# Block attention and a mixture of experts on one core: the first steps reordered, constants on GpSimd, two weight loads on its queue

## The chip, the cores and the metric

The kernel runs on one core of one Trainium2 chip. The metric is the device time of a run in microseconds; the time given is the median of several runs.

## The reference

Attention over q, k, v of shape (4, 8, 768, 64): each query sees the keys within 16 positions and, for each of 24 blocks of 32, one summary (the maximum of the block's keys, with the mean of its values). The result, 3072 tokens of 512, goes through a mixture of 16 experts in 4 groups, one expert for each token.

```python
k_sum = k.reshape(B, H, nb, block, D).max(axis=3)
v_sum = v.reshape(B, H, nb, block, D).mean(axis=3)
scores_l = where(abs(i - j) < 16, scale * q @ k.T, -1e9)
scores_s = scale * q @ k_sum.T + log(32)
a = softmax(concat([scores_l, scores_s]))
x = a @ concat([v, v_sum])           # then (B*S, H*D)
g = argmax(x @ w_group); e = argmax(x @ w_expert[g])
out = p_g * p_e * (relu(x @ w1[g, e]) @ w2[g, e])
```

## The kernel before

**Attention.** The 32 heads are worked on in 16 pairs, `idx`; a pair takes three steps `n`, with four tiles of 64 queries from each head. `PLAN` (line 49) lists, for each of the three steps, the pieces of work in their order: `s` the scores (eight products on TensorE, then a mask pass `ss` on VectorE, L794), `e` the exponentials on ScalarE (L803), `t` the transposes of the probabilities of two steps before, `v` the products with the values of three steps before, `p0` to `p4` the preparation of k and q of the next pair (`prep`, L740: `p0`, `p1` transpose k, with copies into `kw` on ScalarE and VectorE, L763; `p2`, `p3` transpose q into `qt` on ScalarE, L757; `p4` copies the borders and reduces the block maxima on VectorE, L771 to L777), `m0` and `m1` the means of the values (`means`, L720) and `l0` to `l3` the routing logits of pairs further back. Each engine works through its own instructions in the order in which they were written, and the scores of the first step of a pair need all of its `p` pieces.

`means` in its first part multiplies the 12 value tiles with the matrix `stair`; 24 rows of block means result in `vp`. Its second part multiplies `vp` with `same`, which copies the means to the partitions from 96 on, and six GpSimd copies (L737) put them into the value tile `va`. Row 120 of `va` holds zeros, set once for each of the four buffers by `init_last` on GpSimd (L676).

**Loads.** `load_qk` (L629) loads k and q of a pair in one DMA each of 384 KB, `load_vw` the values in six DMAs (two of 192 KB, four of 44 KB) in pieces of 256 bytes. SyncE issues all of these. At the start it issues k and q of the pairs 0 and 1, the values of 0 and 1, and k and q of 2. `keep_warm` (L655) puts products with zeros on TensorE. For the steps 0 to 2 the means of pair 0 are written behind the step: after `n` = 1 its first part, after `n` = 2 its second. After `n` = 0 come the value memsets of the other three buffers and `router.consts` (L163), which makes the constants of the routing, `lower`, `ones` and `seen` by VectorE among them.

**Experts.** Tokens are gathered by indirect DMAs that GpSimd issues (L1041), and written by scatters (L1081). Weights come by `load_w` (L1012) in two halves of 1 MB: w1 (`w1r`) and w2 (`w2r`), both issued by SyncE. They are split into a high and a low part: a cast on ScalarE (`w1h`, `w2h`, L1034) and a subtraction on VectorE. `hook` in `block_attention_then_moe` (L1357) starts the first region while attention still runs: the first gathers at step last - 4, w2 at last - 2. The unit region follows: `weights` loads w1 and w2 of unit 0 once its number is known, `tokens` then issues the gathers of `xd` (`gather2(0)`) and, later, those of `ohr` (`gather2(1)`). `logits` copies the transposed tokens into `xT` (L847): part 0 on ScalarE, part 1 on VectorE.

Of the kernel before, what the change touches and what calls it, by code (L numbers as in the profile page):

```python
# [8 lines left out]
F32 = mybir.dt.float32  # L9
# [5 lines left out]
ALU = mybir.AluOpType  # L15
# [35 lines left out]
        ["s", "p3", "l3", "t", "v", "l0", "m0", "e"]]  # L51
LAG = {"l0": 1, "l1": 2, "l2": 2, "l3": 2}
# [10 lines left out]
GATHER_AT, W2_AT, X_AT = 4, 2, 1  # L63
# [6 lines left out]
AHEAD, LATE_AHEAD, SLOT_AHEAD, VECTOR_NS = 300, 1500, 800, 85  # L70
# [64 lines left out]
class Router:  # L135
# [27 lines left out]
    def consts(self):  # L163
# [12 lines left out]
        V.tensor_single_scalar(self.lower, self.lower, 0.0, op=ALU.is_gt)  # L176
        self.ones = pool.tile([P, P], BF16, name="ones")
        V.memset(self.ones, 1.0)
# [3 lines left out]
        self.ioe = iota([P, E], [[1, E]], -E, 0, "ioe")  # L182
        self.io32 = iota([32, E], [[1, E]], 0, 0, "io32")
# [8 lines left out]
        V.memset(self.seen, 0.0)  # L192
# [181 lines left out]
    def slots(self, name, col, nt, step, c0):  # L374
# [7 lines left out]
        def columns(values):  # L382
# [3 lines left out]
            for j0, eq in zip(groups, eqs):  # L386
# [8 lines left out]
                yield from self.pause(SLOT_AHEAD)  # L395
# [190 lines left out]
def attention(tc, q, k, v, w_group, w_expert, ident, x_dram, ps, router, hook):  # L586
# [24 lines left out]
    with ExitStack() as st, ExitStack() as nat_st:  # L611
# [62 lines left out]
        def init_last(i):  # L674

            nc.gpsimd.memset(va_ring[i][96:NR, :, :, 0:D], 0.0)  # L676

        for i in range(NVA):
            init_va(i)
        qk[1] = load_qk(1)  # L680
        load_vw(0)
        init_last(0)
# [4 lines left out]
        for cs, key in ((slice(0, QT), 0), (before, -PAD), (behind, QT)):  # L687
            nc.gpsimd.iota(mask[:, 0, cs], pattern=[[1, cs.stop - cs.start]], base=key, channel_multiplier=0,
                           allow_small_or_imprecise_dtypes=True)
        pi = cst.tile([P, 3], I32, name="place_i")  # L690
# [27 lines left out]
        same = cst.tile([P, NBLK], F32, name="same")  # L718

        def means(idx, part):  # L720
# [10 lines left out]
            else:  # L731
                T.matmul(out=t[KW:NC, 0:P], lhsT=same, rhs=vps.pop(idx), start=True, stop=True)
                vr = wk.tile([NC, 1, 2, D], F32, name="vr")
                V.tensor_copy(out=vr[KW:NC].rearrange("p a h d -> p (a h d)"), in_=t[KW:NC, 0:P])  # L734
                n = 2
                for i in range(0, NQT, n):
                    nc.gpsimd.tensor_copy(out=va[KW:NC, i:i + n, :, 0:D], in_=vr[KW:NC].broadcast_to([NBLK, n, 2, D]))  # L737
# [99 lines left out]
        def logits(idx, part):  # L837
            b, a = order[idx]
            x = xs[b]
            if part < 2:  # L840
# [6 lines left out]
                (V.tensor_copy if part else nc.scalar.copy)(  # L847
# [27 lines left out]
        keep_warm(5)  # L875
# [5 lines left out]
        for i in range(4):  # L881
            V.tensor_copy(out=same[32 * i:32 * i + 32], in_=ident[32 * i:32 * i + 32, 32 * i:32 * i + NBLK])
# [5 lines left out]
        for n in range(NG + 3):  # L888
# [4 lines left out]
            for step in PLAN[g]:  # L893
# [10 lines left out]
                elif step[0] == "m" and n < NG:  # L904
                    j = idx + (step == "m0")
                    if 0 < j < len(order):
                        means(j, int(step[1]))
                elif step[0] == "l" and 0 <= idx - LAG[step] < len(order):
                    logits(idx - LAG[step], int(step[1]))
            if n == 0:  # L910
                for i in range(1, NVA):
                    init_last(i)
# [536 lines left out]
```

## Time and profile before

| | |
|---|---|
| median of 3 runs | 520.9 us (520.44 to 521.11) |
| the profiled execution | 521.21 us, its span 519.5 us |
| mean granted TensorE clock | 0.986 |
| busy: PE, PEld | 491.7 us (95%), 415.4 us (80%) |
| busy: DVE, ACT, POOL | 359.4 us (69%), 317.3 us (61%), 120.8 us (23%) |
| DMA | 106.95 MB, 206 GB/s in the mean |

PE is TensorE, PEld its weight loads, DVE VectorE, ACT ScalarE, POOL GpSimd and SP SyncE (SPq its DMA queue). Times count from the start of the span. A busy time says how long the instructions of an engine ran; where an engine waited, the brackets of a timeline row give how long it had been idle and what ended that.

### The profile page before, as it was taken

The page shows a single profiled execution, that of the slowest core. Times are in us where ns is not written, and L with a number is a line of the kernel's source. Part 1 is how long each engine was busy: PE and PEld are TensorE (multiplying, and loading weights), DVE is VectorE, ACT ScalarE, POOL GpSimd, SP SyncE. Part 2 cuts the span into 40 slices and gives each one's busy share as a digit, 9 for nine tenths or more (in the row PEclk, how much of TensorE's full clock was granted, in tenths as well). Part 3 has the DMA queues.
Part 4 walks back from the last instruction along what each step waited for, and adds up shares of the span by engine and source line. Part 5 has one row for each costly group of instructions (what it writes and reads, how often), then busy time and mean ns, then how long its engine had stood idle before and what let it go on. Part 6 is the DMA issues. An engine that isn't in the chain of part 4 may idle for free.

```text
span 519.5 us, 13330 instructions
## 1 busy us (share of the span) xinstructions
PE 491.7 (95%) x4966; PEld 415.4 (80%) x4966; DVE 359.4 (69%) x1090; ACT 317.3 (61%) x596; POOL 120.8 (23%) x200
## 2 busy tenths in 40 slices
PE   7799999999999899999999999999999999999993
PEld 4677767777777688978898989898898989897772
DVE  7687899888977978877746546473736546483782
ACT  5599888888988643216645546473645546474681
POOL 7313112211312400035020202022130202023232
PEclk9799999999999899999999999999999999999998
DMA  9998767888747530196996666765565756754890
GB/s 170 180 194 170 147 137 211 172 151 199 175 115 260 201 123 21 26 374 194 414 378 249 245 229 220 258 222 189 202 243 208 272 206 211 260 209 130 281 361 29
DMA packets 76341, 106.95 MB, mean 206 GB/s; under 512 B 40286, under 2 KB 40366, under 8 KB 76256
## 3 DMA queue, kind: packets, MB, share of 16 engines
q1 hardware_dynamic: 71296, 90.98, 60.6%
q0 software_dynamic: 4960, 14.92, 7.8%
q8 instruction: 43, 0.70, 0.6%
q14 instruction: 42, 0.34, 0.2%
HBM read 97.49 MB, written 13.24 MB: 213 GB/s over the span
## 4 chain that ended last, share of the span: by engine, by line
PE 69%; DVE 15%; issue 9%; ACT 3%; DMA 2%; POOL 1%; POOLq 0%; DVEq 0%; ACTq 0%
PE ps_s L120 41%; PE ps_av L120 15%; PE ps_tr L120 12%; DVE ss L794 3%; DVE ks L774 2%; DVE kw L763 2%; ACT kw L763 1%; DMA xd<-x_dram,t_unit_gather 1%; DVE w1l L120 1%; DVE kw L771 1%; PE ps_lg L658 1%; DVE kw L777 1%; DVE kw L772 1%; DMA out_dram<-y,t_unit_scatter 1%; ACT qt L757 1%
## 5 line engine op out<-in xcount | busy, mean ns | idle before, releaser
L120 DVE TENSOR_TENSOR w2l<-w2r,w2h 128x1024 fp32r<-128x1024 f32 x52 | 63.3, 1225 | 77.4 <-ACT w2h L1034 77.4
L120 PE MATMUL ps_s<-xT,w1h 128*128 128x256 f32 x448 | 83.5, 285 | 0.0
L120 PEld LDWEIGHTS ps_s<-xT,w1h 128*128 128x128 f32 x448 | 70.8, 192 | 0.9 <-issue 0.6
L1081 POOL DMA_INDIRECT out_dram<-y,t_unit_scatter x24 | 24.7, 1027 | 192.6 <-ACT y L1076 112.9
L120 PE MATMUL ps_s<-xT,w1l 128*128 128x256 f32 x224 | 63.4, 283 | 0.0
L803 ACT ACTIVATE pr<-ss,nm 128x120 f32<-128x120 f32 x192 | 60.1, 387 | 4.7 <-DVE nm L794 4.3
L737 POOL COPY va<-vr 24x256 f32<-24x256 f32 x96 | 34.7, 405 | 120.6 <-DVE vr L734 114.7
L120 DVE TENSOR_TENSOR w1l<-w1r,w1h 128x1024 fp32r<-128x1024 f32 x52 | 60.4, 1220 | 3.3 <-ACT w1h L1034 3.3
L1119 ACT ACTIVATE hTh<-ps_s 128x512 fp32r<-128x512 f32 x48 | 28.7, 598 | 53.7 <-PE ps_s L120 33.1
L120 PE MATMUL ps_s<-ohr,w1h 128*128 128x256 f32 x320 | 58.9, 283 | 0.0
L1034 ACT CAST w2h<-w2r 128x1024 fp32r<-128x1024 f32 x52 | 53.8, 1041 | 1.2 <-DVE w1l L120 0.6
L1034 ACT CAST w1h<-w1r 128x1024 fp32r<-128x1024 f32 x52 | 50.7, 1052 | 0.0
L120 PEld LDWEIGHTS ps_s<-ohr,w1h 128*128 128x128 f32 x320 | 49.8, 188 | 0.2
L120 DVE SCALAR_TENSOR_TENSOR hTl<-ps_s,hTh 128x512 fp32r<-128x512 f32 x48 | 33.1, 691 | 24.1 <-ACT hTh L1119 23.5
L794 DVE CUSTOM_DVE_ANT_0 ss<-mask,ps_s 128x120 f32<-128x120 f32 x192 | 42.1, 274 | 4.4 <-PE ps_s L120 3.6
L120 PE MATMUL ps_s<-ohr,w1l 128*128 128x256 f32 x160 | 45.0, 281 | 0.0
L120 PE MATMUL ps_s<-kw,qt 64*64 64x120 f32 x768 | 38.4, 282 | 5.9 <-DVE nm L794 5.1
L120 PEld LDWEIGHTS ps_s<-xT,w1l 128*128 128x128 f32 x224 | 43.0, 192 | 0.3
L120 PE MATMUL ps_s<-w2h,hTh 128*128 128x512 f32 x104 | 41.7, 401 | 0.0
L120 PE MATMUL ps_av<-w2h,hTh 128*128 128x512 f32 x104 | 41.6, 400 | 0.0
L120 PE MATMUL ps_s<-w2h,hTl 128*128 128x512 f32 x104 | 41.1, 395 | 0.0
L120 PE MATMUL ps_av<-w2l,hTh 128*128 128x512 f32 x104 | 41.1, 395 | 0.0
(275 smaller groups left out, 1013.4 us busy)
## 6 DMA issues: line engine op xcount, KB each, us to landing
w2r<-in_moe_w_dram SPq DMA_DIRECT2D x32, 1024.0 KB, 7.1
w1r<-in_moe_w_dram SPq DMA_DIRECT2D x30, 1024.0 KB, 8.1
kn<-in_k_dram SPq DMA_DIRECT2D x16, 384.0 KB, 3.8
qn<-in_q_dram SPq DMA_DIRECT2D x16, 384.0 KB, 5.7
va<-in_v_dram SPq DMA_DIRECT2D x32, 192.0 KB, 4.2
x_dram<-xt SPq DMA_DIRECT2D x12, 512.0 KB, 7.2
va<-in_v_dram SPq DMA_DIRECT2D x64, 44.0 KB, 4.2
w_first<-in_moe_w_dram SPq DMA_DIRECT2D x2, 1024.0 KB, 4.7
```

Source lines behind the costliest of these rows:

```text
L120: return f(*args, **kw)
L658: nc.tensor.matmul(out=t, lhsT=zero, rhs=zero[:, None, :].broadcast_to([P, 4, P]), start=True, stop=True)
L737: nc.gpsimd.tensor_copy(out=va[KW:NC, i:i + n, :, 0:D], in_=vr[KW:NC].broadcast_to([NBLK, n, 2, D]))
L757: nc.scalar.activation(out=out[:, j], in_=tv.rearrange("p i t r -> p t i r"), func=AF.Copy, scale=-1.0 / 8.0)
L763: (nc.scalar.copy if j == 0 or h and idx in ACT_K1 else V.tensor_copy)(out=out[:, j], in_=tv.rearrange("p i t r -> p t r i"))
L771: V.tensor_copy(out=kw[:, 1:NQT, before], in_=kw[:, 0:NQT - 1, QT - PAD:QT])
L774: V.reduce_max(out=ks, axis=AX.X, in_=kw[:, :, 0:QT].rearrange("p t (a k) -> p t a k", k=BLOCK))
L794: V.tensor_tensor_reduce(out=ss[:, u], in0=mask[:, 1 if t == 0 else 2 if t == NQT - 2 else 0], in1=sp[h][:, j], scale=1.0, scalar=3.4e38, ...
L803: nc.scalar.activation(out=pr[:, i, 0:NC], in_=sp[:, i], func=AF.Exp, bias=nm[:, i:i + 1], scale=-1.0)
L1034: self.nc.scalar.copy(out=h, in_=src)
L1081: self.nc.gpsimd.indirect_dma_start(out=self.out, out_offset=bass.IndirectOffsetOnAxis(ap=self.tabs[name, "scatter"][0:y.shape[0], col:col ...
L1119: nc.scalar.activation(out=th[:, js], in_=hp, func=AF.Relu)
```

## The change

The loads of the values of pair 0 are written ahead of those of k and q of pair 1. The first four steps get an order of their own, `START`, with the means of pair 0 as `m0` and `m1`, those of pair 1 as `n0`, and four products to keep TensorE warm, `w`; five such products ahead of step 0 become nine. `same` is made by GpSimd, with a 25th column; the product with it yields a 25th row, of zeros, which goes into `va` with the others, and `init_last` is gone. `ones` is set by GpSimd, and `lower` and `seen` are finished by a function of their own after step 4. The w2 loads of the first region and of unit 0 are issued by GpSimd, the former at last - 4, behind the first gathers, the latter behind the gathers of `xd`. The xT copy of part 1 goes to ScalarE for the last pair. `pause` gets another distance in one place, which leaves the order of every engine as it is.

```diff
--- before.py
+++ after.py
@@ -49,6 +49,8 @@
 PLAN = [["s", "p0", "l1", "t", "v", "p1", "e", "p4"],
         ["s", "p2", "t", "v", "m1", "l2", "e"],
         ["s", "p3", "l3", "t", "v", "l0", "m0", "e"]]
+START = [["s", "e"], ["s", "m0", "e"], ["s", "w", "t", "m1", "p0", "p1", "e", "p4", "p2", "p3"],
+         ["t", "v", "s", "n0", "p0", "p1", "e", "p4"]]
 LAG = {"l0": 1, "l1": 2, "l2": 2, "l3": 2}
 
 T_LAG, V_LAG = 2, 3
@@ -60,14 +62,14 @@
 
 
 W1_AT = 34
-GATHER_AT, W2_AT, X_AT = 4, 2, 1
+GATHER_AT, X_AT = 4, 1
 SPLIT_AT = (-4, -3, -2, -1)
 FIRST = {1: 2, 2: 1, 3: 1}
 
 XT_AT = 4
 
 
-AHEAD, LATE_AHEAD, SLOT_AHEAD, VECTOR_NS = 300, 1500, 800, 85
+AHEAD, LATE_AHEAD, SLOT_AHEAD, WEIGHT_AHEAD, VECTOR_NS = 300, 1500, 800, 3000, 85
 
 
 class Banks:
@@ -173,14 +175,13 @@
         self.row = iota([32, 1, 1], [[0, 1], [0, 1]], 0, 1, "row")
 
         self.lower = iota([P, E, E], [[1, E], [-1, E]], 0, 0, "lower")
-        V.tensor_single_scalar(self.lower, self.lower, 0.0, op=ALU.is_gt)
+        self.ioe = iota([P, E], [[1, E]], -E, 0, "ioe")
+        self.io32 = iota([32, E], [[1, E]], 0, 0, "io32")
         self.ones = pool.tile([P, P], BF16, name="ones")
-        V.memset(self.ones, 1.0)
+        nc.gpsimd.memset(self.ones, 1.0)
         self.tri = pool.tile([P, P], BF16, name="tri")
         nc.gpsimd.affine_select(out=self.tri, in_=self.ones, pattern=[[1, P]], compare_op=ALU.is_gt, fill=0.0,
                                 base=0, channel_multiplier=-1)
-        self.ioe = iota([P, E], [[1, E]], -E, 0, "ioe")
-        self.io32 = iota([32, E], [[1, E]], 0, 0, "io32")
         self.is_m = pool.tile([P, E], F32, name="is_m")
         self.eoh = pool.tile([P, NT, E], F32, name="eoh")
         self.q = pool.tile([P, NT], F32, name="q_all")
@@ -189,7 +190,10 @@
         self.big = pool.tile([P, 1], F32, name="big")
         self.taken = pool.tile([P, E], F32, name="taken")
         self.seen = pool.tile([P, E], F32, name="seen")
-        V.memset(self.seen, 0.0)
+
+    def compared(self):
+        self.V.tensor_single_scalar(self.lower, self.lower, 0.0, op=ALU.is_gt)
+        self.V.memset(self.seen, 0.0)
 
     def pause(self, ahead=None):
 
@@ -392,7 +396,7 @@
                 for i, v in enumerate(values):
                     V.tensor_tensor(out=bo[:, :, i], in0=eq, in1=bc(v[:, js], n), op=ALU.mult)
                     yield
-                yield from self.pause(SLOT_AHEAD)
+                yield from self.pause(SLOT_AHEAD if values[0] is self.tok1 else WEIGHT_AHEAD)
                 if j0 == 0:
                     t = self.ps["tr" if nt == step else "lg"].next()
                     sl = t[0:m, 0:P] if swap else t[:, 0:m]
@@ -671,15 +675,11 @@
             V.memset(va[96:NR, :, :, D:D + 1], EPS)
             V.memset(va[0:NC, :, :, D:D + 1], 1.0)
 
-        def init_last(i):
-
-            nc.gpsimd.memset(va_ring[i][96:NR, :, :, 0:D], 0.0)
-
-        for i in range(NVA):
+        init_va(0)
+        load_vw(0)
+        qk[1] = load_qk(1)
+        for i in range(1, NVA):
             init_va(i)
-        qk[1] = load_qk(1)
-        load_vw(0)
-        init_last(0)
 
         place = cst.tile([P, 3], F32, name="place")
         nc.gpsimd.iota(place[:, 0:1], pattern=[[0, 1]], base=0, channel_multiplier=1, allow_small_or_imprecise_dtypes=True)
@@ -687,6 +687,9 @@
         for cs, key in ((slice(0, QT), 0), (before, -PAD), (behind, QT)):
             nc.gpsimd.iota(mask[:, 0, cs], pattern=[[1, cs.stop - cs.start]], base=key, channel_multiplier=0,
                            allow_small_or_imprecise_dtypes=True)
+        same = cst.tile([P, NBLK + 1], F32, name="same")
+        for i in range(4):
+            nc.gpsimd.tensor_copy(out=same[32 * i:32 * i + 32], in_=ident[32 * i:32 * i + 32, 32 * i:32 * i + NBLK + 1])
         pi = cst.tile([P, 3], I32, name="place_i")
         V.tensor_copy(out=pi[:, 0:1], in_=place[:, 0:1])
         V.tensor_scalar(out=pi[:, 1:2], in0=pi[:, 0:1], scalar1=RUN - 1, scalar2=3, op0=ALU.bitwise_and,
@@ -715,8 +718,6 @@
         for i in range(2):
             V.memset(stair[BLOCK * i:BLOCK * i + BLOCK, NBLK - 2 + i:NBLK - 1 + i], 1.0 / BLOCK)
 
-        same = cst.tile([P, NBLK], F32, name="same")
-
         def means(idx, part):
 
             va = va_ring[idx % NVA]
@@ -729,12 +730,12 @@
                 vps[idx] = sm.tile([P, P], F32, name="vp", bufs=2)
                 V.tensor_copy(out=vps[idx], in_=t[:, 0:P])
             else:
-                T.matmul(out=t[KW:NC, 0:P], lhsT=same, rhs=vps.pop(idx), start=True, stop=True)
-                vr = wk.tile([NC, 1, 2, D], F32, name="vr")
-                V.tensor_copy(out=vr[KW:NC].rearrange("p a h d -> p (a h d)"), in_=t[KW:NC, 0:P])
+                T.matmul(out=t[KW:NR, 0:P], lhsT=same, rhs=vps.pop(idx), start=True, stop=True)
+                vr = wk.tile([NR, 1, 2, D], F32, name="vr")
+                V.tensor_copy(out=vr[KW:NR].rearrange("p a h d -> p (a h d)"), in_=t[KW:NR, 0:P])
                 n = 2
                 for i in range(0, NQT, n):
-                    nc.gpsimd.tensor_copy(out=va[KW:NC, i:i + n, :, 0:D], in_=vr[KW:NC].broadcast_to([NBLK, n, 2, D]))
+                    nc.gpsimd.tensor_copy(out=va[KW:NR, i:i + n, :, 0:D], in_=vr[KW:NR].broadcast_to([NBLK + 1, n, 2, D]))
 
 
         def prep(idx, part):
@@ -844,7 +845,7 @@
                 tp = ps_tr.next()
                 for i in range(n):
                     T.transpose(out=tp[:, i * P:(i + 1) * P], in_=x[:, j0 + i, a * P:(a + 1) * P], identity=ident)
-                (V.tensor_copy if part else nc.scalar.copy)(
+                (V.tensor_copy if part and idx < len(order) - 1 else nc.scalar.copy)(
                     out=xTs[idx][:, j0:j0 + n].rearrange("p c r -> p (c r)"), in_=tp[:, 0:n * P])
             elif part == 2:
 
@@ -872,14 +873,12 @@
 
         for part in (0, 1, 4, 2, 3):
             prep(0, part)
-        keep_warm(5)
+        keep_warm(9)
         for t in prr:
             V.memset(t[:, :, NC:NR], 1.0)
         load_vw(1)
         qk[2] = load_qk(2)
 
-        for i in range(4):
-            V.tensor_copy(out=same[32 * i:32 * i + 32], in_=ident[32 * i:32 * i + 32, 32 * i:32 * i + NBLK])
         nc.gpsimd.memset(wcat[:, :, 20:32], 0.0)
         nc.gpsimd.dma_start(out=wcat[:, :, 0:4], in_=w_group.rearrange("(a p) g -> p a g", p=P))
         for i in range(G):
@@ -890,7 +889,7 @@
             if n < NG:
                 b, a = order[idx]
                 xs[b] = x_ring[b % 2]
-            for step in PLAN[g]:
+            for step in START[n] if n < len(START) else PLAN[g]:
                 if step == "s" and n < NG:
                     sps = scores(n)
                 elif step == "e" and n < NG:
@@ -902,17 +901,19 @@
                 elif step[0] == "p" and n < NG and idx + 1 < len(order):
                     prep(idx + 1, int(step[1]))
                 elif step[0] == "m" and n < NG:
-                    j = idx + (step == "m0")
-                    if 0 < j < len(order):
+                    j = idx + (step == "m0" and n > 2)
+                    if (j > 0 or n < 3) and j < len(order):
                         means(j, int(step[1]))
+                elif step == "w":
+                    keep_warm(4)
+                elif step == "n0":
+                    means(1, 0)
                 elif step[0] == "l" and 0 <= idx - LAG[step] < len(order):
                     logits(idx - LAG[step], int(step[1]))
             if n == 0:
-                for i in range(1, NVA):
-                    init_last(i)
                 router.consts()
-            elif n < 3:
-                means(0, n - 1)
+            elif n == 4:
+                router.compared()
             if n in ROUTE_AT:
                 b1 = ROUTE_AT.index(n)
                 work.append(router.route(b1 * TB, (b1 + 1) * TB))
@@ -1011,7 +1012,7 @@
 
     def load_w(self, row, which, cond=None, queue=None):
         queue = queue or self.nc.sync
-        e = self.entry(row, [ET.SP if queue is self.nc.sync else ET.Activation])
+        e = self.entry(row, [ET.SP if queue is self.nc.sync else ET.Pool])
         kw = {} if cond is None else dict(cond=cond)
         src, dst = (self.w1f, self.w2f)[which], self.raw(row, which)
         n = dst.shape[1] // 2
@@ -1337,6 +1338,7 @@
 
 
 def block_attention_then_moe(tc, q, k, v, w_group, w_expert, w1, w2, out):
+    nc = tc.nc
     with ExitStack() as st:
         const = st.enter_context(tc.tile_pool(name="const", bufs=1))
         dram = st.enter_context(tc.tile_pool(name="dram", bufs=1, space=DRAM))
@@ -1365,9 +1367,7 @@
             if n == last - GATHER_AT:
                 need(2)
                 ex.gather1(0)
-            if n == last - W2_AT:
-
-                ex.load_w(("first", 0), 1)
+                ex.load_w(("first", 0), 1, queue=nc.gpsimd)
             if n == last - X_AT:
                 ex.x_t1()
                 if NE > 2:
@@ -1398,13 +1398,13 @@
         def weights():
             while not router.ready & 1:
                 yield
-            for which in range(2):
-                ex.load_w(("unit", 0), which)
+            ex.load_w(("unit", 0), 0)
 
         def tokens():
             while not router.ready & 2:
                 yield
             ex.gather2(0)
+            ex.load_w(("unit", 0), 1, queue=nc.gpsimd)
             yield
 
             while not router.ready & 4:
```

TensorE at the start, from the warming products to the second pair's first scores. `ps_s<-kw,qt` is a score product (eight in a step), `stair` the first part of the means, `same` the second, `pr` the probabilities, `ident,kn` and `ident,qn` the transposes of k and q; rows that repeat are left out. Before:

```order
L120 MATMUL ps_s_66<-kw_135,qt_133 64x120
L120 MATMUL ps_tr_64<-ident,kn 128x96 x4
L120 MATMUL ps_tr_63<-ident,qn 128x96 x4
L120 MATMUL ps_tr_64<-va_109,stair 32x128 x12
L120 MATMUL ps_tr_65<-ident,qn 128x96 x4
L120 MATMUL ps_tr_63<-ident,pr_187 121x128 x4
L120 MATMUL ps_tr_64<-va_110,stair 32x128 x12
L120 MATMUL ps_tr_65<-vp,same 24x128
L120 MATMUL ps_s_66<-kw_136,qt_134 64x120
```

and with the change:

```order
L122 MATMUL ps_s_66<-kw_135,qt_133 64x120
L122 MATMUL ps_tr_64<-va_109,stair 32x128 x12
L122 MATMUL ps_s_67<-kw_135,qt_133 64x120
L662 LDWEIGHTS zero
L122 MATMUL ps_tr_65<-ident,pr_191 121x128 x4
L122 MATMUL ps_tr_63<-vp,same 25x128
L122 MATMUL ps_tr_64<-ident,kn 128x96 x4
L122 MATMUL ps_tr_63<-ident,qn 128x96 x4
L122 MATMUL ps_tr_65<-ident,pr_192 121x128 x4
L122 MATMUL ps_av_69<-va_109,ptS 64x65 x8
L122 MATMUL ps_s_66<-kw_136,qt_134 64x120
```

The stair products of the first values stand ahead of the second pair's transposes of k and q now, with four warming products (`zero`) behind the third step's scores; `same` has 25 columns, and the first product with the values (`ps_av`) comes ahead of the second pair's scores.

SyncE at the start; `kn` and `qn` are k and q of a pair, `va_109` to `va_111` the value buffers of the pairs 0 to 2. Before:

```order
L629 DMA kn<-in_k_dram 96x2x512
L629 DMA qn<-in_q_dram 96x2x512
L629 DMA kn<-in_k_dram 96x2x512
L629 DMA qn<-in_q_dram 96x2x512
L643 DMA va_109<-in_v_dram 64x12x64 x2
L643 DMA va_109<-in_v_dram 16x11x64 x4
L643 DMA va_110<-in_v_dram 64x12x64 x2
```

and with the change:

```order
L633 DMA kn<-in_k_dram 96x2x512
L633 DMA qn<-in_q_dram 96x2x512
L647 DMA va_109<-in_v_dram 64x12x64 x2
L647 DMA va_109<-in_v_dram 16x11x64 x4
L633 DMA kn<-in_k_dram 96x2x512
L633 DMA qn<-in_q_dram 96x2x512
L647 DMA va_110<-in_v_dram 64x12x64 x2
```

The second k and q, which stood ahead of the first values, stand behind them.

GpSimd between the first region and unit 0: `xd` and `ohr` are gathers of the unit's tokens, `y` the rows that are written out; the second w2r load, like the first, is left out. Before:

```order
L1081 DMA out_dram<-y_3487,t_first_scatter 3072x512
L1041 DMA xd<-x_dram,t_unit_gather 128x512 x2
L1081 DMA out_dram<-y_3488,t_first_scatter 3072x512
L1041 DMA ohr<-x_dram,t_unit_gather 128x512 x2
L1041 DMA xg_3095<-x_dram,t_unit_gather 128x512
```

and with the change:

```order
L1082 DMA out_dram<-y_3491,t_first_scatter 3072x512
L1042 DMA xd<-x_dram,t_unit_gather 128x512 x2
L994 TENSOR_LOAD t_unit
L1021 ISA
L1021 DMA w2r_3482<-in_moe_w_dram 128x4x512
L1082 DMA out_dram<-y_3492,t_first_scatter 3072x512
L1042 DMA ohr<-x_dram,t_unit_gather 128x512 x2
L1042 DMA xg_3099<-x_dram,t_unit_gather 128x512
```

Two w2 loads, each with a small instruction ahead of it, stand between the gathers of `xd` and the scatter and the gathers of `ohr`.

## Rows read from the trace of the kernel before

**Rows 1.** Chain of waits, 0 to 60 us: start, us, what.

```profile
27.80 0.28 DVE ss L794
...
37.54 0.28 DVE ss L794
```

**Rows 2.** Window 240 to 260 us: each engine busy (instructions), PEclk, DMA share, GB/s.

```profile
240.00:260.00 20.00, 20.00 (x141) 18.49 (x140) 14.68 (x16) 12.51 (x17) 5.09 (x4) 1.00 0.90 343
```

**Rows 3.** Timeline 0 to 30 us: start, us, engine line instruction xcount [idle before].

```profile
7.25 1.24 PE L658 MATMUL ps_lg<-zero 128*128 128x512 bf16 x5
...
10.57 4.10 POOL L676 MEMSET va<- 25x1536 f32 x3
...
11.55 1.25 ACT L803 ACTIVATE pr<-ss,nm 128x120 f32<-128x120 f32 x4
...
13.30 1.49 DVE L772 COPY kw<-kw 128x176 f32<-128x176 f32 x1
...
15.16 0.98 PE L120 MATMUL ps_tr<-va,stair 96*32 96x128 f32 x24 [2.94 <-DMA va<-in_v_dram]
...
15.90 0.28 DVE L120 TENSOR_SCALAR lower<-lower 128x256 f32<-128x256 f32 x1
...
21.52 1.08 PE L120 MATMUL ps_s<-kw,qt 64*64 64x120 f32 x16
...
24.44 0.55 PE L120 MATMUL ps_tr<-ident,kn 96*128 96x96 f32 x4
...
24.91 0.64 PE L120 MATMUL ps_s<-kw,qt 64*64 64x120 f32 x16
25.02 0.50 ACT L763 COPY kw<-ps_tr 64x384 f32<-64x384 f32 x1 [0.51 <-PE ps_tr L120]
...
25.55 0.56 DVE L763 COPY kw<-ps_tr 64x384 f32<-64x384 f32 x1 [0.26 <-ACT kw L763]
...
26.32 0.24 DVE L772 COPY kw<-kw 128x176 f32<-128x176 f32 x1
...
26.70 0.97 ACT L757 ACTIVATE qt<-ps_tr 64x384 f32<-64x384 f32 x2
```

**Rows 4.** Window 17 to 18 us, columns as in rows 2.

```profile
17.00:18.00 1.00, 1.00 (x15) 0.70 (x16) 0.47 (x5) 0.96 (x4) 0.00 (x0) 0.50 1.10 165
```

**Rows 5.** DMA, 0 to 40 us: GB/s moved in each 1 us slice.

```profile
GB/s 0 23 309 283 250 231 260 210 163 150 148 112 66 94 151 173 154 165 254 227 230 134 155 171 187 252 236 224 160 150 164 204 299 255 202 142 147 151 189 240
```

**Rows 6.** Single loads by tile: third qn, then the two halves of w1r.

```profile
L629 SPq DMA_DIRECT2D qn<-in_q_dram x1: 313/313/313, 15.0 to 15.0; - x1
...
DMA to landing us min/median/max: 7.7/7.7/7.7
...
L1020 SPq DMA_DIRECT2D w1r<-in_moe_w_dram x2: 383/386/388, 219.4 to 220.0; - x2
...
DMA to landing us min/median/max: 8.1/8.1/8.1
```

**Rows 7.** Timeline, 187 to 189.5 us.

```profile
188.25 0.41 DVE L847 COPY xT<-ps_tr 128x256 f32<-128x256 f32 x1
...
188.81 0.53 PE L120 MATMUL ps_lg<-xT,wcat 128*32 128x192 f32 x8 [1.03 <-DVE ri L120]
```

**Rows 8.** Timeline, 229 to 249 us: POOL, PE and ACT.

```profile
229.57 1.04 POOL L1041 DMA_INDIRECT xd<-x_dram,t_unit_gather  x1 [0.31 <-issue]
...
235.04 1.13 PE L120 MATMUL ps_tr<-identr,xd 128*128 128x128 f32 x8 [0.94 <-DMA xd<-x_dram,t_unit_gather]
...
241.76 1.05 ACT L1034 CAST w2h<-w2r 128x1024 fp32r<-128x1024 f32 x1 [0.55 <-DVE w1l L120]
...
246.73 1.04 ACT L1034 CAST w2h<-w2r 128x1024 fp32r<-128x1024 f32 x1
...
247.48 0.79 PE L120 MATMUL ps_tr<-identr,ohr 128*128 128x128 f32 x8
```

**Rows 9.** Direct loads that GpSimd issues, by tile (wcat).

```profile
L886 POOL DMA_DIRECT2D wcat<-in_moe_w_expert_dram x4: 787/787/820, 7.5 to 9.7; - x4
```

## The prediction

> **What bounds the kernel now.** I read the busy tenths first: PE is busy 95% of the span, so a gain can only come from stretches in which it waits or runs at its lower clock. The windows show where that is not so: from 240 to 260 us PE is busy 20.00 of 20 us at full clock [rows 2], and the MoE goes on like this to the end. The attention before it has a fixed period: the chain of waits passes the first mask pass `ss` of one head pair at 27.80 us and that of the next at 37.54 us, 9.74 us later [rows 1]. A gain before 27.80 us therefore shifts everything behind it, and nothing else in this stage is touched.
>
> At the start the timeline shows the loss. PE stands idle for 2.94 us until 15.16 us, because the stair products of the means wait for the first value load [rows 3]. The scores of idx 0 are queued behind them. After this idle time the granted clock is 0.50, the lower of its two levels (1.2 against 2.4 GHz) [rows 4], and a score group takes 1.08 us at 21.52 us, against 0.64 us at 24.91 us [rows 3].
>
> The MoE has two small waits: 1.03 us at 188.81 us, behind an xT copy on DVE [rows 7], and 0.94 us at 235.04 us, for the first gather of tokens of a unit [rows 8].
>
> **The change, part by part.** *Start.* The first values move ahead of the second k and q. From 2 us on the DMA moves 250 to 309 GB/s, and falls to 66 to 151 GB/s once the values are what is left [rows 5]. The second k and q are 0.79 MB, which at 250 GB/s is 3.1 us. If transfers are served roughly in the order of issue, the values land at about 15.0 - 3.1 = 11.9 us; counted from the front (k and q of idx 0 done near 5 us, then some 0.59 MB at 100 to 150 GB/s) it is 9 to 11 us. I take 11.5 us.
>
> From there the new order gives, with full-clock durations [rows 3]: stair products 0.98, to 12.5; score group of step 2, 0.64, to 13.1; four warming blocks, 4/5 of 1.24, to 14.1; transposes of probabilities (0.55, from the k transposes), to 14.7; the product of means and the first k transposes, to 15.5. Then ACT sets the pace: two kw copies of 0.50 to 16.5, the exponentials of step 2, 1.25 to 17.75, and two times 0.97 for qt to 19.7. DVE makes its part of kw to 18.3 meanwhile, under this cover. So the scores of step 3 start at 19.7 us, where they started at 21.52.
>
> Step 3 then needs the score group (0.64), the stair products of idx 1 (0.98) and eight k transposes (2 x 0.55), to 22.4 us. A kw copy on ACT and one on DVE end at 23.5. Before, the last DVE kw copy ended at 26.11 us (25.55 + 0.56) and `ss` began at 27.80, 1.69 us later [rows 1, 3]. That gives 25.1 us for the new `ss`, against 27.80: **-2.7 us**, bounds -4 (values at 10 us, no wait for loads) and +0.8 (below).
>
> The third k and q are issued no later than before in the queue; the third q took 7.7 us from 15.0, so it landed at 22.7 [rows 6], which is about when its transposes come now. I cost that at nothing, but there is no cover left: a later landing would show one for one.
>
> *Constants.* The copies of `same` go from DVE to GpSimd, in place of a value memset there. The other value memsets are gone: three took 4.10 us from 10.57 on, and beside them the DVE copy L772 took 1.49 us, against 0.24 us at 26.32 [rows 3]. The saving is in the chain above already (DVE is hidden there by ACT). Comparing `lower` and clearing `seen` moves behind step 4. It took 0.28 us on DVE ahead of `ss` [rows 3]; there I bound it by 0 and 0.35 us and take **+0.3**, since in the periodic part `ss` follows DVE directly. The zero row comes out of a product of the same time with 25 columns for 24: nothing.
>
> *xT copy of the last idx.* PE waited 1.03 us; the copy of 0.41 us on DVE began at 188.25 [rows 7]. On ACT it need not queue there. Bounds 0 and -1.0, taken **-0.4**, the length of the copy, since what DVE does next is then the late piece.
>
> *Second weights.* In the unit stage the gather of `xd` was issued to 230.61 (229.57 + 1.04) and PE waited to 235.04 [rows 8], with the second weights, issued by SP just before, ahead of it. Now these are issued after it. The first weights landed at 220.0 + 8.1 = 228.1 us [rows 6], before the gather is issued. So the wait should go: **-0.9**, bound 0. Its price: two issues on GpSimd of 0.79 us, the time of its direct loads [rows 9], ahead of a scatter and the `ohr` gathers, and a later landing. Issued at 231 and 232, 2 MB take about the 8.1 us of the first weights, to 240.3 us; their casts come at 241.76 and 246.73 [rows 8]. With the halves at about 236.2 and 240.3, and all casts 0.9 us earlier, the slack is 4.7 and 5.5 us. I cost it at nothing; if an issue takes longer, that slack is what covers it.
>
> The same move ahead of the first region, which the chain shows no PE wait for, I cost at nothing: cover is the attention that still runs.
>
> The longer pause of the planner (WEIGHT_AHEAD) moves no row of an engine here: nothing.
>
> The sum is -2.7 + 0.3 - 0.4 - 0.9 = **-3.7 us**. The profiled execution took 521.21 us, the median is 520.9; so 517.5 for such an execution, **517.2 us** at the median. A difference of 0.2%, 1.0 us, is what a measurement of this kernel can tell from none.
>
> **Rivals.**
> *The clock falls again (0.22).* PE has little to do between 15.5 and 19.7 us, only transposes, and the stretch before 15.16 shows what idle time led to. For it: 0.50 at 17 us [rows 4]. Against it: PE is never idle for 2.94 us at a stretch. Price, from rows at both levels: two score groups 2 x 0.44, the stair products and transposes some 0.8 more: 1.7 us, so 518.9.
>
> *Loads late (0.06).* SP holds k and q of idx 1 back until earlier loads are done, and those of idx 2 stand behind the next values. Each us past 22.4 costs one; 1.5 us give 518.7.
>
> *The values come no sooner (0.07).* If transfers share the DMA instead of following one another, the values land near 15.0 as before, and the new order, in which all of step 2 stands behind them, takes 8.2 us from there to the scores of step 3: 23.2 against 21.52. The 5.4 us from there to `ss` (19.7 to 25.1 above) give 28.6, +0.8, so 520.9 + 0.8 + 0.3 - 0.4 - 0.9 = 520.7: no change. It decides, between faster and no change, at a landing of about 14.2 us. Against it: the fall in GB/s when k and q are through [rows 5].
>
> *GpSimd's queue becomes the bound (0.07), slower than before.* A direct load was issued in 0.79 us when DVE had little to do [rows 9]. Beside a DVE in full work it may take longer, as L772 took 6 times as long beside GpSimd's memset [rows 3]. Place: the two issues from 230.9 us, with a scatter and two `ohr` gathers (1.35 each: 1.04 and the gap of 0.31) behind them, and 4.4 us from issue to the product that uses them (230.61 to 235.04). At 6 us per issue the second ends at 242.9. `ohr` is there at 242.9 + 3 x 1.35 + 4.4 = 251.4, against 247.48 [rows 8], and the second weights at 242.9 + 8.1 = 251.0, against a cast at 246.73: +4.3 us, so 520.9 - 2.7 + 0.3 - 0.4 + 4.3 = 522.4. It decides at about 5.5 us per issue, where the gains are used up; at 0.79 us it has 5 us of slack.
> The Trainium skill, "SBUF — State Buffer", section "A bandwidth-pool intuition that's wrong (but worth ruling out)", says that a DMA whose descriptors GpSimd writes takes some 3100 ns beside a DVE tensor_copy and 620 ns alone, since the two engines lock a shared port against each other. By that factor of 5 an issue would take, by estimate, 4 us, and with a gain in the unit region used up the total would be about 518. The slow L772 beside GpSimd's memset agrees with a shared port, but no row here shows such an issue beside a busy DVE.
>
> **How the numbers follow.** My forecast has 0.58, its own range 515.6 to 518.2. To hold 8 in 10, the range takes in the fallen clock and late loads and leaves out the two cases above 520: **515.4 to 519.4**. Faster by over 0.2% (below 519.9): the forecast, the clock, the loads, less a margin for errors in several steps: 0.82. Within: 0.10. Slower: 0.08.
>
> **What would show it.** In the new profile: no PE idle time near 3 us at 12 to 15; values landed by 12; scores of step 3 near 19.7 and `ss` of step 4 near 25.1; granted clock 1.0 from 15 to 25 (0.5 if the clock rival holds); L772 near 0.25 us; no wait for `xd` near 234; the wait before `ps_lg` near 187 shorter by 0.4; two w2r issues of about 0.8 us on GpSimd and no w2h cast waiting for a DMA. A first value load that lands near 15, or issues above 4 us, would make the prediction wrong.

## The result and the profile after

The changed kernel takes 516.33 us in the median of 7 runs (513.89 to 518.9), against 521.11 for the kernel before beside it: a ratio of 0.9895 (95% interval 0.9858 to 0.9932), 4.8 us less. The profiled execution took 515.85 us, its span is 514.2 us, PE busy for 492.2 us. Its runs spread over 5 us; the sections below show two sources of that.

The timeline of the changed kernel at the start:

```profile
11.32 0.86 PE L122 MATMUL ps_tr<-va,stair 96*32 96x128 f32 x24
...
18.70 0.39 PE L122 MATMUL ps_s<-kw,qt 64*64 64x120 f32 x2 [0.63 <-DVE kw L778]
19.24 1.07 PE L122 MATMUL ps_s<-kw,qt 64*64 64x120 f32 x14 [0.15 <-ACT qt L758]
...
26.10 0.28 DVE L795 CUSTOM_DVE_ANT_0 ss<-mask,ps_s 128x120 f32<-128x120 f32 x1
```

The stair products start at 11.32 us with no wait, where they waited 2.94 us until 15.16 [rows 3]; the scores of step 3 come from 18.70 us on, for 21.52. But the mask pass of step 4 comes at 26.10 for 27.80 [rows 1], only 1.70 us earlier, since the clock fell here too (windows of the same kernel; busy times, the clock third from the right):

```profile
16.00:18.00 2.00, 1.79 (x24) 1.42 (x24) 1.94 (x5) 1.96 (x7) 1.08 (x4) 1.00 1.19 142
18.00:20.00 2.00, 1.22 (x20) 0.89 (x16) 1.13 (x4) 1.74 (x4) 0.00 (x0) 0.75 1.04 256
20.00:22.00 2.00, 2.00 (x32) 1.31 (x27) 1.00 (x9) 0.00 (x0) 0.00 (x0) 0.50 1.36 174
22.00:24.00 2.00, 2.00 (x24) 1.64 (x22) 0.89 (x3) 1.15 (x3) 0.00 (x0) 0.50 1.39 154
```

The later places, from its timeline (PE, POOL):

```profile
186.31 0.53 PE L122 MATMUL ps_lg<-xT,wcat 128*32 128x192 f32 x8 [0.46 <-ACT xT L848]
...
227.07 1.04 POOL L1042 DMA_INDIRECT xd<-x_dram,t_unit_gather  x1 [0.30 <-issue]
228.11 1.63 POOL L1021 DMA_DIRECT2D w2r<-in_moe_w_dram  x2
...
231.20 0.40 PE L122 MATMUL ps_s<-w2h,hTl 128*128 128x512 f32 x1
231.43 0.80 PE L122 MATMUL ps_tr<-identr,xd 128*128 128x128 f32 x8
232.07 0.47 PE L122 MATMUL ps_s<-w2h,hTh 128*128 128x512 f32 x1
```

The products on either side of the `xd` transposes before the change:

```profile
233.70 0.40 PE L120 MATMUL ps_s<-w2h,hTl 128*128 128x512 f32 x1
...
236.00 0.47 PE L120 MATMUL ps_s<-w2h,hTh 128*128 128x512 f32 x1
```

The wait ahead of `ps_lg` is 0.46 us for 1.03 [rows 7], the wait for `xd` (0.94, [rows 8]) is gone, and the two w2r issues on GpSimd take 1.63 us together. From the product ahead of the `xd` transposes to the one behind them it is 0.87 us now, for 2.30: 1.43 us less, of which the wait ahead of them is the larger part; the eight transposes themselves went on over 1.13 us before and 0.80 now.

How far ahead of the kernel before the profiled executions are, at six points in the order of the program (us; the same instruction in both; minus is earlier; the points of the kernel before are 27.80, 166.2, 186.65, 191.0, 243.4 and 511.2 us). Late attention is a mask pass near the end of the attention, `hTh` the high part of the hidden values of an expert, written by ScalarE, and `y` the rows of the result. At two places the clock of the kernel before is down itself, from some 16.5 to 23.3 us and from some 177 to 180 us.

| kernel | mask pass, step 4 | late attention | first hTh | second hTh | unit hTh | last y |
|---|---|---|---|---|---|---|
| changed | -1.70 | -1.50 | -1.94 | -2.50 | -3.94 | -3.78 |
| e1 (the same) | -1.70 | -1.46 | -2.47 | -3.02 | -4.48 | -4.96 |
| e9 (the same) | -2.92 | -2.84 | -3.19 | -3.76 | -5.20 | -5.16 |
| e4 loads back | +3.93 | +3.98 | +3.29 | +2.72 | +1.27 | +0.81 |
| e5 steps back | +0.38 | +0.38 | +0.17 | -0.40 | -0.41 | -0.26 |
| e10 loads and steps back | -0.77 | -0.71 | -1.28 | -1.85 | -3.30 | -3.25 |
| e11 start only | -2.71 | -2.62 | -1.67 | -1.67 | -1.72 | -1.70 |
| e6 unit w2 by SyncE | -2.48 | -2.45 | -3.05 | -3.62 | -4.05 | -3.82 |
| e7 first w2 by SyncE | -3.09 | -3.02 | -3.19 | -3.77 | -5.20 | -5.18 |
| e8 xT on VectorE | -1.32 | -0.43 | -1.04 | -1.04 | -2.51 | -2.33 |
| e2 four more warming products | -2.61 | -2.59 | -3.59 | -4.16 | -5.62 | -6.10 |
| e3 sixteen more | -0.21 | -0.17 | +0.68 | +0.11 | -1.34 | -1.79 |
| e12 six more | -2.30 | -2.22 | -2.62 | -3.19 | -4.65 | -4.58 |

From the last y to the end of the span an execution takes 6.8 to 9.7 us, and the same kernel differs in it: the last scatter waits until the one before it has landed, and GpSimd is idle for 3.02 us in the changed kernel and 4.94 in e1. So the points of the table tell the parts apart better than the times.

### The profile page after: what moved, and what is told of

Same layout as the page of the kernel before. It is cut to its first block, busy times and chain, and to the rows that moved or that the text cites. A ratio compares the mean times of both kernels' runs of the same rounds, so it can differ in the third digit from the quotient of the medians.

```text
span 514.2 us, 13346 instructions
## 1 busy us (share of the span) xinstructions
PE 492.2 (96%) x4974; PEld 415.5 (81%) x4974; DVE 356.6 (69%) x1084; ACT 317.8 (62%) x597; POOL 120.9 (24%) x205
## 4 chain that ended last, share of the span: by engine, by line
PE 49%; issue 19%; DMA 12%; DVE 11%; ACT 3%; POOL 3%; POOLq 1%; DVEq 0%; ACTq 0%
PE ps_s L122 26%; DMA out_dram<-y,t_unit_scatter 12%; PE ps_tr L122 12%; PE ps_av L122 10%; DVE ss L795 3%; DVE ks L775 2%; DVE kw L764 1%; ACT kw L764 1%; PE ps_lg L122 1%; POOL ohr L1042 1%; ACT qt L758 1%; PE ps_lg L662 1%; POOLq L1185 1%; ACT pr L804 1%; DVE kw L778 1%
## 5 line engine op out<-in xcount | busy, mean ns | idle before, releaser
L738 POOL COPY va<-vr 25x256 f32<-25x256 f32 x96 | 35.9, 418 | 118.8 <-DVE vr L735 118.8
```

Of the source, the lines that this page charges most:

```text
L738: nc.gpsimd.tensor_copy(out=va[KW:NR, i:i + n, :, 0:D], in_=vr[KW:NR].broadcast_to([NBLK + 1, n, 2, D]))
```

## The experiments

All edits are against the changed kernel, lines left out are marked `...`, and the ratios are against the kernel before, measured beside each run. An expectation names a theory and a rival; the text behind it says which of them held.

**The same kernel again, e1 and e9.** No edit.

> The changed kernel unaltered. Theory: the granted clock falls to 0.50 near 19 us each time, since TensorE has the same gaps between 15 and 19 us; first mask pass of step 4 at 26.1 us as in the first profile, time about 516.3 us. Rival: the fall in that one profile was chance; then the mask pass comes near 24.5 to 25 us, the clock stays at 1.0 from 15 to 26 us, and the time is about 515.

> The changed kernel unaltered, beside the two halves of it. Theory (the same instructions at the start meet a clock that falls in some executions and not in others): first mask pass of step 4 either at 24.7 to 25.4 us with the clock at 1.0 from 16 to 27 us, or at 26.0 to 26.5 us with some 7 us at 0.50; nothing between; median near 516 to 517. Rival (each kernel has one course): 26.10 us again.

e1: 517.36 us, ratio 0.9883 (0.9849 to 0.9918). e9: 515.39, 0.9896 (0.9864 to 0.9928). In e1 the clock fell as in the first profile; in e9 it stayed at 1.0, and the mask pass came at 24.88 us (windows, then timeline of e9):

```profile
18.00:20.00 2.00, 1.21 (x28) 0.78 (x28) 1.22 (x5) 1.75 (x4) 0.00 (x0) 1.00 1.06 252
20.00:22.00 2.00, 1.81 (x44) 1.43 (x40) 1.11 (x9) 0.49 (x1) 0.00 (x0) 1.00 1.35 177
22.00:24.00 2.00, 1.83 (x38) 1.45 (x28) 1.89 (x5) 1.95 (x7) 0.00 (x0) 1.00 1.38 164
```

```profile
20.87 0.88 PE L122 MATMUL ps_tr<-ident,kn 96*128 96x96 f32 x8 [0.19 <-DMA kn<-in_k_dram]
...
22.49 0.52 PE L122 MATMUL ps_tr<-ident,qn 96*128 96x96 f32 x4 [0.17 <-DMA qn<-in_q_dram]
...
24.88 0.28 DVE L795 CUSTOM_DVE_ANT_0 ss<-mask,ps_s 128x120 f32<-128x120 f32 x1
```

Until 18 us the first profile and that of e9 agree (PE busy 1.79 of 2.00 from 16 to 18 in both); then the clock fell in one and not in the other. Of the seven profiles with this start (changed, e1, e6 to e9, e11) three fell, the third one (e8) only near 21 us, behind a wait of 0.79 us for the second values. Where it stayed up the mask pass came at 24.7 to 25.3 us, where it fell at 26.1 to 26.5. The rival, one course for each kernel, falls, and with it the theory that I had for e1. The rows of e9 show the next limit: TensorE now waits for the third k and q.

**Warming products in the gaps, e2, e3, e12.** The third and fourth list of `START`; a number behind `w` is the number of products.

```diff
 e2:
-["s", "w", "t", "m1", "p0", "p1", "e", "p4", "p2", "p3"], ["t", "v", "s", "n0", "p0", "p1", "e", "p4"]
+["s", "w", "t", "m1", "p0", "p1", "e", "p4", "p2", "w2", "p3"], ["t", "v", "w2", "s", "n0", "p0", "p1", "e", "p4"]
 e3:
+["s", "w", "t", "m1", "p0", "p1", "w4", "e", "p4", "p2", "w4", "p3"], ["t", "w4", "v", "w4", "s", "n0", "p0", "p1", "e", "p4"]
 e12:
+["s", "w", "t", "m1", "p0", "p1", "e", "p4", "p2", "w2", "p3"], ["t", "v", "w2", "s", "n0", "w1", "p0", "p1", "w1", "e", "p4"]
```

> Two warming products between the two q transposes of step 2 and two ahead of the scores of step 3, in gaps of 0.45 and 0.63 us in which TensorE was idle. Theory (these gaps let the clock fall): no stretch at 0.50 between 15 and 27 us, first mask pass of step 4 at 24.4 to 25.0 us against 26.1, and 1.1 to 1.7 us less time than the changed kernel. Rival (the clock falls for another reason than these gaps): 0.50 from about 19 us to 25 as before, mask pass at 26.0 to 26.4, same time as the changed kernel.

> Sixteen warming products in the same stretch (four each behind the k transposes, between the q transposes, behind the transposes of probabilities and behind the value products); 4 us of added TensorE work, of which the gaps take 1.1 to 1.8. Theory (gaps let the clock fall): clock 1.0 from 15 to 27 us, scores of step 3 no later than 20.0 us, mask pass of step 4 at 24.6 to 25.8, time 0.3 to 1.5 us below the changed kernel. Rival: the clock falls all the same and the added products cost their time, mask pass at 26.5 to 28, time up to 2 us above the changed kernel.

> The kernel of e2 (two warming products between the q transposes of step 2 and two ahead of the scores of step 3) with one more ahead of the k transposes of step 3 and one behind them. Theory (gaps let the clock fall; filling them costs nothing): clock at 1.0 from 15 to 27 us, mask pass of step 4 at 24.7 to 25.5 us, mean clock of the timed runs at 0.990 or more as in e2 and e3, median 1.0 to 1.5 us below the unaltered kernel. Rival (e2 and e3 were lucky executions): the same spread of clocks and times as the unaltered kernel.

e2: 516.36, 0.9863 (0.9832 to 0.9895). e3: 516.17, 0.9847 (0.9812 to 0.9883). e12: 515.42, 0.9894 (0.9863 to 0.9926). In none of the three profiles did the clock fall between 15 and 27 us, as expected, but neither did it in four of the seven without them. Beside e1 the runs of e2 and e3 have a mean granted clock of 0.992 against 0.988; beside e9, with the same clock of 0.992, e12 gains nothing. None can be told from the unaltered kernel: inconclusive. The mask pass came at 25.19 us in e2 (24.4 to 25.0 expected) and at 25.50 in e12. That of e3 came at 27.59 us, later than expected, but its scores of step 0 were 1.6 us late already (last section).

**The start taken apart, e4 and e5.**

```diff
 e4:
         init_va(0)
-        load_vw(0)
         qk[1] = load_qk(1)
+        load_vw(0)
 e5:
-            for step in START[n] if n < len(START) else PLAN[g]:
+            for step in PLAN[g]:
...
+            elif n < 3:
+                means(0, n - 1)
```

> The changed kernel with the loads in their old order: k and q of pair 1 ahead of the first values. Theory (the early values carry the gain of the start): the values land near 15 us, the stair products of pair 0 wait for them, the scores of step 3 start at 21.8 to 23.2 us against 18.7, and the mask pass of step 4 comes at 27.5 to 29 us; 1.5 to 2.9 us above the changed kernel, 518 to 519. Rival (the order of the steps carries it): scores of step 3 before 20 us and the same time as the changed kernel.

> The changed kernel with the steps in their old order (the plan of the later steps from step 0 on, the means of pair 0 behind steps 1 and 2); the values are still loaded early. Theory (early values and new order are one change, since k and q of pair 1, which land at 11.5 and 13.1 us now, are needed by the old order right behind step 0): TensorE waits for k at 10 to 11.5 us and for q to 13, first mask pass of step 4 at 26.3 to 27.8 us, 0.3 to 1.7 us above the changed kernel. Rival (the load order alone is what gains): mask pass of step 4 at 26.1 us or before, and the time of the changed kernel or less.

e4: 523.32 us, 0.9999 (0.9977 to 1.0021): the whole gain is gone. The theory holds, with too small a price: the loss of 5.6 us at the mask pass is twice the most that was expected. The values were awaited until 16.10 us (timeline of e4), all of step 2 stood behind them, and the clock was at 0.50 from 16 to 20 us:

```profile
16.10 1.63 PE L122 MATMUL ps_tr<-va,stair 96*32 96x128 f32 x24 [4.71 <-DMA va<-in_v_dram]
...
21.20 0.40 PE L122 MATMUL ps_tr<-vp,same 128*25 128x128 f32 x2
...
26.36 0.63 PE L122 MATMUL ps_s<-kw,qt 64*64 64x120 f32 x14 [0.16 <-ACT qt L758]
```

e5: 518.78 us, 0.9929 (0.9901 to 0.9956); the mask pass came at 28.18 us, 0.38 later than before the change. The rival falls; the theory holds in its sense, but not in its bounds. The waits for k and q were short (0.21 and 0.17 us), the next values were awaited until 19.49 us, and the clock fell here too:

```profile
12.00 0.88 PE L122 MATMUL ps_tr<-ident,kn 96*128 96x96 f32 x8 [0.21 <-DMA kn<-in_k_dram]
...
13.62 0.55 PE L122 MATMUL ps_tr<-ident,qn 96*128 96x96 f32 x4 [0.17 <-DMA qn<-in_q_dram]
...
16.50 0.63 PE L122 MATMUL ps_s<-kw,qt 64*64 64x120 f32 x14 [1.19 <-DVE nm L795]
...
19.49 1.63 PE L122 MATMUL ps_tr<-va,stair 96*32 96x128 f32 x24 [0.82 <-DMA va<-in_v_dram]
```

Its step 0 was late by some 1.7 us too, as in e3. How much of the 28.18 us comes from that no run separates, since the wait for the next values stands behind it. At the mask pass, the order without the loads is 3.9 us behind the kernel before, the loads without the order are 0.4 us behind it in this one execution, and together they are 2.5 to 3.1 ahead where the clock stays up. e10, below, has neither.

**The other parts taken back, e6, e7, e8.**

```diff
 e6:
             ex.load_w(("unit", 0), 0)
+            ex.load_w(("unit", 0), 1)
...
-            ex.load_w(("unit", 0), 1, queue=nc.gpsimd)
 e7:
-                ex.load_w(("first", 0), 1, queue=nc.gpsimd)
+            if n == last - 2:
+                ex.load_w(("first", 0), 1)
 e8:
-                (V.tensor_copy if part and idx < len(order) - 1 else nc.scalar.copy)(
+                (V.tensor_copy if part else nc.scalar.copy)(
```

> The changed kernel with w2 of unit 0 issued by SyncE behind w1 again. Theory (the gather of xd waits behind these 2 MB): TensorE waits about 0.9 us for xd again near 231 us, and everything behind it comes 1.4 us later than in the changed kernel against the same point near 220 us; time 1.0 to 1.5 us above the changed kernel. Rival (the 1.4 us that the changed kernel gains between 220 and 245 us come from elsewhere, such as less traffic at the time): no wait for xd and the same shift as in the changed kernel.

> The changed kernel with w2 of the first region issued by SyncE at step last - 2 again. Theory (the move gains nothing of itself, as predicted): the shift against the kernel before is the same just before 165 us and at the first hTh near 185 us, within 0.3 us of the changed kernel's, same time. Rival (the gathers that land earlier, and with them the value copies of GpSimd, give the 0.4 to 1.0 us that the changed kernel gains between these points): that gain is gone, time 0.4 to 1.0 us above the changed kernel.

> The changed kernel with the last xT copy on VectorE again. Theory (the copy queues on VectorE): the wait ahead of ps_lg near 186 us is about 1.0 us again instead of 0.46, and the shift between the first and the second hTh is 0.55 us worse; time 0.4 to 0.6 us above the changed kernel. Rival (the shorter wait came with the earlier weights): wait near 0.5 us, same shift.

e6: 518.14 us, 0.9939 (0.9916 to 0.9962). TensorE waits 0.55 us for `xd`, and between the second hTh and the unit's the profile gains 0.43 us, where the others gain 1.43 to 1.47 (e5, with a fallen clock at 232 to 236 us, left aside). The move is worth 1.0 us here and 1.4 by e11. The theory holds; by the ratios e6 is 2.2 to 2.9 us above the changed kernel, but the intervals overlap.

e7: 518.48 us, 0.9928 (0.9899 to 0.9958). By the table the gain between late attention and the first hTh is 0.17 us here; with the load on GpSimd it is 0.2 to 1.0, but e3, which has the load there too, loses 0.85. There is a wait that the changed kernel lacks (timeline of e7):

```profile
172.60 0.51 PE L122 MATMUL ps_tr<-identr,xg 128*128 128x128 f32 x4 [0.75 <-DMA xg<-x_dram,t_first_gather]
```

By the ratios the time is some 2 us above the changed kernel's, but the intervals overlap. The clock was down between 173 and 178 us here. It fell near this place in all three profiles with the load on SyncE (before, e7, e11, which lost 0.95 us there) and in five of the eleven with the load on GpSimd (changed, e3, e4, e5, e12). What this move is worth, between nothing and 2 us, stays open.

e8: 516.55 us, 0.9892 (0.9859 to 0.9925). The wait ahead of `ps_lg` is 1.03 us again and the gain between the two hTh is 0.00, against 0.55 to 0.57 in all kernels with the copy on ScalarE. The theory holds; in the median 0.56 us does not show.

**The halves, e10 and e11.** e10 has the edits of e4 and e5 together, e11 those of e6, e7 and e8.

> The changed kernel with both the loads and the steps of the start in their old order; the weight loads on GpSimd, the xT copy and the constants stay changed. Theory (parts add up): mask pass of step 4 at 27.5 to 28.5 us as before the change, then 0.3 to 0.35 us lost in step 4, 0.56 us gained at the xT copy and 1.0 to 1.4 us in the unit region: 1.5 to 2.5 us less than the kernel before. Rival (the weight loads gain only where the start is early): less than 0.8 us below the kernel before.

> The changed kernel with w2 of both regions issued by SyncE again and the last xT copy on VectorE; only the start and the constants stay changed. Theory (parts add up): mask pass of step 4 at 24.7 to 25.4 or at 26.0 to 26.5 us, the wait of 1.0 us ahead of ps_lg and a wait of 0.5 to 0.9 us for xd there; 1.4 to 3.0 us less than the kernel before, 1.5 to 2.5 us above the changed kernel. Rival (the early start is lost again later, at a point that is fixed by transfers): no more than 0.8 us below the kernel before.

e10: 517.79 us, 0.9936 (0.9909 to 0.9963). That is 3.4 us less than the kernel before, more than the 1.5 to 2.5 expected, and its mask pass came at 27.03 us, half a microsecond sooner than expected; the rival falls. e11: 518.84 us, 0.9953 (0.9932 to 0.9975), 2.3 us less than the kernel before, as expected; it is some 3 to 3.6 us above the changed kernel by the ratios, where 1.5 to 2.5 was expected. Its rival falls too. The two gains, 0.64% and 0.47%, make 1.11%, beside 1.05 to 1.17% for the changed kernel: the parts add up, as far as intervals of 0.2 to 0.3% on each can say.

e10, e4, e5 and the changed kernel differ in the start alone: neither part 0.9936, the order alone 0.9999, the loads alone 0.9929, both 0.9883 to 0.9896. The order alone loses 0.6%, clear of the intervals; the loads alone change nothing that the times show; both together gain 0.4 to 0.5%, though here the intervals overlap.

In e11 the wait for `xd` is back (timeline):

```profile
233.51 0.94 PE L122 MATMUL ps_tr<-identr,xd 128*128 128x128 f32 x8 [1.12 <-DMA xd<-x_dram,t_unit_gather]
```

## Why the prediction was right

517.2 us was forecast and 516.33 measured, inside the range. By its steps:

- **Start, -2.7 us.** The values landed before 11.3 us (11.5 taken), the scores of step 3 started at 18.70 (19.7 forecast), and with the clock up the mask pass came at 24.7 to 25.3 us (25.1 forecast): -2.5 to -3.1. (The slices of rows 5 from 2 to 8 us read 210 to 309 GB/s, not 250 to 309; at 210 the landing would be worked out at 11.3 us for 11.9, which changes nothing in the sum.) So near a hit is in part luck: the way to the scores was 1.0 us shorter than I had it, and the way from there to the mask pass took 6.0 to 6.6 us instead of 5.4. In the first profile the clock rival took part of the gain: -1.70. I gave that rival 0.22, and it came in three of seven profiles. Its price was 1.7 us; at the mask pass the fall cost 1.2 (24.88 in e9 against 26.10 in e1), and by late attention e8 is 2.0 to 2.6 behind the four in which the clock stayed up. It belongs to the execution, not to the kernel, so it is no separate case but a part of the spread.
- **Third k and q, nothing, with no cover left.** The missing cover was right, the price of nothing a little low: of the four profiles in which the clock stayed up, TensorE waited for k in three (e9, e6, e11: 0.19 to 0.41 us) and for q in two (e9 0.17, e6 0.46). The mask pass came at 24.71 us in e7, with neither wait, and at 25.32 in e6, with the longest.
- **`lower` and `seen`, +0.3 us.** Failed: step 5 comes 0.35 us later, but where the clock stayed up nothing is left of it one step on (ahead of the kernel before by 2.92 in e9 at the mask passes of step 4, by 2.57 of step 5, by 2.91 of step 6; 2.71, 2.36 and 2.70 in e11). Nothing was the right price; TensorE set the pace there: the mask pass of step 6 waits for its scores (VectorE idle for 0.19 us until 29.62 us in e9).
- **The constants, in the chain already.** The border copy that took 1.49 us beside GpSimd's memset takes 0.23 to 0.24 now. e10, with the old loads and steps, has its mask pass 0.77 us earlier than before, but the constants have not brought its scores of step 3 forward: they start at 21.53 us, for 21.52 before. What differs is the clock, which is at 1.00 from 22 to 24 us there, for 0.67 before, so that these scores take 0.64 us for 1.08 [rows 3] (timeline of e10):

```profile
21.53 0.64 PE L122 MATMUL ps_s<-kw,qt 64*64 64x120 f32 x16
```

Whether the edits or the execution brought the clock back sooner no run separates.
- **xT copy, -0.4 us.** -0.56, shown by e8 and e11.
- **Second weights, -0.9 us.** -1.0 to -1.4, shown by e6 and e11. I had bounded it by the one wait ahead of the `xd` transposes; the rest is at the same place, in the transposes: from the product ahead of them to the one behind it was 1.43 us longer before, which is the whole gain.
- **First region, nothing.** 0.2 to 1.0 us of gain in most rows of the table, a loss of 0.85 in e3; open, as said at e7.
- **The longer `pause`, nothing.** It stands in the changed kernel and in all of e1 to e12, so no run separates it.
- **GpSimd's queue as the bound.** Excluded. The four w2r issues took 816 to 837 ns, also from 167.9 to 169.6 us, where VectorE was busy for 1.70 of 1.70 us (windows of the changed kernel):

```profile
167.90:169.60 1.70, 1.58 (x31) 1.08 (x30) 1.70 (x10) 1.64 (x4) 1.66 (x3) 1.00 0.70 239
```

The factor of 5 that the Trainium skill, "SBUF — State Buffer", section "A bandwidth-pool intuition that's wrong (but worth ruling out)", gives for such a DMA beside a tensor_copy does not appear. VectorE did subtractions, mask passes and a small copy here, and the issue took about what it took at the start, 787 to 820 ns [rows 9].

The prediction is wrong on those rows: VectorE did not have "little to do" beside them, and a row of a busy VectorE was there. It was busy for 2.92 of the 3.00 us from 7.5 to 10.5 us, with copies inside SBUF among it (timeline of the kernel before):

```profile
7.49 3.04 POOL L886 DMA_DIRECT2D wcat<-in_moe_w_expert_dram  x4
...
9.14 0.16 DVE L882 COPY same<-ident 32x24 f32<-32x24 f32 x1
...
9.31 1.22 DVE L882 COPY same<-ident 32x24 f32<-32x24 f32 x3
```

So the trace of before already spoke against this rival. It was VectorE that was slow there: three copies took 1.22 us together and ended with the last issue, where one took 0.16.

- **Values no sooner.** Excluded by the stair products at 11.32; e4 shows what it would have cost: +3.9 us at the mask pass against the kernel before, where I had worked out +0.8. The values came 1.1 us later there than the 15.0 I had taken, the way from them to the scores of step 3 took 9.7 us instead of 8.2, with the clock at 0.50 for half of it, and the rest 5.9 instead of 5.4.

The range held, but the gain was forecast too small: the three measurements of the changed kernel gain 4.8, 6.4 and 5.8 us for 3.7. At the last y the changed kernel is 5.2 us ahead in e9, where the clock stayed up: 2.9 from the start, 0.3 in the first region, 0.6 by the xT copy and 1.4 by the weights. In the first profile it is 3.8 us ahead, since the fall of the clock gave back what the other terms gained over the forecast; that this is so near 3.7 is chance.

## What to carry to other kernels

An order of loads and an order of steps that uses them are one change: price them together, and expect no gain from either alone. Here the order alone lost 0.6%, and the loads alone changed nothing that the times show. A gather that a busy engine waits for belongs ahead of a big load that is needed 10 us later, even if the load must move to another queue. Where single executions spread by more than a part is worth, compare the same instructions in the profiles, point by point, and count the falls of the clock before a difference is put down to an edit.

## What the runs showed of the hardware

The granted clock of one and the same program fell or stayed up after the same instructions (e1 and e9, at 19 us), for some 7 us, 1.2 us of time; a similar fall between 173 and 186 us comes in some executions and not in others. In e3 the nine warming products ahead of step 0 took 3.29 us, in the first profile 2.11, while the clock reads 1.00 in both (timelines, e3 first):

```profile
7.79 3.29 PE L662 MATMUL ps_lg<-zero 128*128 128x512 bf16 x9
```

```profile
7.03 2.11 PE L662 MATMUL ps_lg<-zero 128*128 128x512 bf16 x9
```

So a slow stretch can also stand in the durations alone. All of these executions begin slowly: the first eight warming products, from 1.1 or 1.2 us on, take 3.2 to 3.6 us, where nine take 2.11 later, also with the clock shown as 1.00. In the others the durations have come down by some 7 us, in e3 and e5 only near 11 us, with TensorE busy for at least 1.92 of every 2.00 us from 2 to 10 us in both. What makes the clock fall in one execution and not in the next, or the first stretch longer, no run here shows.
